# A Fourier-mixing and gated-MLP kernel on one core: moments in 32-byte pieces, merged down stores, and sums moved to the first stage

## The chip, the core and the metric

The kernel runs on one core of one Trainium2 chip. A core has a matrix engine (TensorE, PE in the profile, with its weight loads listed as PEld), a vector engine (VectorE, DVE), a scalar engine (ScalarE, ACT), a general engine (GpSimd, POOL) and a sync engine (SyncE, SP). SP and POOL issue nearly all transfers between the chip's memory and the core's buffers; the transfers themselves run on 16 DMA engines. The metric is device time in microseconds (us) of one execution; the median of three runs before the change is 836.01 us (834.29 to 838.94).

## The reference

With x of 2048 rows and 512 columns, in single precision:

```
xn = (x - mean(x)) / sqrt(var(x) + 1e-5)           # over the 512 columns
a, b = xn @ dft_hid_re.T, xn @ dft_hid_im.T        # 512 x 512 matrices
s  = dft_seq_re @ a - dft_seq_im @ b               # 2048 x 2048 matrices
h  = sigmoid(xn @ w_gate) * (xn @ w_up)            # 512 x 1792 each
g  = silu(h @ w_down)                              # 1792 x 512
out = x + s * g
```

All matrices are inputs; nothing is taken to be a Fourier matrix by its values.

## The kernel before

**Arithmetic.** A single-precision product is made of three matmuls on a rounded high part and the rest: high by high, high by low, low by high (`mm3`, L66). ACT makes the high part by a copy to the rounded type (L118), DVE the low part by a subtraction (L123). On top of that each large product is done as a 2 x 2 block product in seven instead of eight multiplications; the sums of blocks which that needs are made on DVE (`combine`, L127). The seven products carry the numbers 1 to 7. Operand data lies in 54 buffers of 4 KB per partition, called pages. A page is given out again when its last reader is done, so a store that has not landed keeps its page.

**Stages.** The work is a list of units, 12 matmuls of 512 columns each, or 18 where a product of the down projection rides along. Two units before a unit runs, its operands are split; five units before, they are loaded. Helper work is hung on unit numbers: `sooner` ahead of the unit, `after` behind it, `amid` between. Each engine takes its instructions in the order so written, and so do the SP and POOL queues.

1. Sequence transform (units 0 to 111): four chunks of 512 output rows. Chunks 0 and 1 share their first two products, unit by unit, while x is loaded, its row moments are computed (`stats`, L156) and x is normalised in place (`normalise`, L173). `stats` runs two statistics instructions on DVE for a tile, then on POOL variance plus epsilon, the power -1/2, the negated mean and the bias. The `moments` go to memory for later use (`store_moments`, L178) in eight transfers of single floats. The results, 16 blocks, go to memory as `f_raw` (L273).
2. Gate and up, with down (98 units from number n = 112): 14 blocks, each a half of the 2048 rows by a 256-wide group of hidden columns. `x_norm` (L424) normalises the transposed x with moments that are read back and broadcast to all partitions (L433, 16 instructions of 1024 columns). The seven down products of a block ride on the units that follow, in the order 2, 1, 6, 7, 4, 5, 3, into two `pd` banks. After each, `gather` (L473) copies both banks to a page on ACT (L477) and POOL stores the page to `g_part` in memory, adding to what is there (L479, or L482 where it is the first). Products 2 and 1 go to the same `g_part`.
3. Hidden transform and output (28 units): it multiplies sums of `f_raw` blocks by sums of the hidden matrices, then scales by silu of `g_part` and adds to the output. The sums are made during stage 2 and go through memory: `f_sums` (L640) at units n+40, n+52, n+64 and n+76, `w_sums` (L660) at n+84. Each `f_sums` loads four blocks, makes four sums on DVE and stores four; `w_sums` likewise. Left-over down products ride along here too.

Of the kernel before, what the change touches and what calls it, by code (L numbers as in the profile page):

```python
# [8 lines left out]
F32 = mybir.dt.float32  # L9
F32R = mybir.dt.float32r  # L10
AF = mybir.ActivationFunctionType
ALU = mybir.AluOpType
# [20 lines left out]
def fnet_glu_kernel(ctx: ExitStack, tc: tile.TileContext, x, x_t, c_re, c_im, w_h, w_gu, w_down, out):  # L33
# [122 lines left out]
    def stats(j, pp):  # L156
        mv = stat.tile([P, 2, 2], F32, name="mv")
        rs = stat.tile([P, 2], F32, name="rs")
        each = [slice(0, 1), slice(1, 2)] if pp == j == 0 else [slice(0, 2)]
        for e in range(2):  # L160
            st = stat.tile([P, 6], F32, name="st")
            nc.vector.bn_stats(st, xs[j, pp][:, e, :])
            nc.vector.bn_aggr(mv[:, e, :], st)
        for at in each:
            scale = moments[:, 1, pp, at, j]
            nc.gpsimd.tensor_scalar(rs[:, at], mv[:, at, 1], EPS, None, op0=ALU.add)
            nc.gpsimd.tensor_tensor(scale, rs[:, at], mhalf[:, at], op=ALU.pow)
        mean, scale, bias = (moments[:, m, pp, :, j] for m in range(3))
        nc.gpsimd.tensor_scalar(mean, mv[:, :, 0], -1.0, None, op0=ALU.mult)
        nc.gpsimd.tensor_tensor(bias, mean, scale, op=ALU.mult)  # L170
        return mv

    def normalise(j, pp, es=(0, 1), d=None):  # L173
        for e in es:
            v = xs[j, pp][:, e, :] if d is None else a_block(d, j, pp)[:, e]
            nc.scalar.activation(v, v, AF.Identity, scale=moments[:, 1, pp, e, j : j + 1], bias=moments[:, 2, pp, e, j : j + 1])
# [48 lines left out]
    class Chunk:  # L225
# [29 lines left out]
        def run(self, k, pp):  # L255
            ch = CHAIN[k]
            if k in (1, 5) and pp == 0:
                self.chain(ch)
            wv, xv = aop[k, pp].get(), self.op[k, pp].get()
            order = [(d, e) for d in range(2) for e in range(2)]  # L260
            if (k, pp) == (1, 0) and self.t < 2:
                order.sort(key=lambda v: v[1])
            late = (self.t, k, pp) == (1, 1, 0)
            for lows in ((0, 1), (2,)) if late else ((0, 1, 2),):
                for d, e in order:
                    ws = [v[:, e, d * P : (d + 1) * P] for v in wv]
                    first, last = k in (1, 5) and pp == e == 0, pp == 3 and e == 1
                    mm3(self.ps[ch, d], ws, [v[:, e, :] for v in xv], first, last, k not in (1, 5), late, lows)
            if pp == 3:
                self.done(k)  # L270

# [43 lines left out]
    def begin_seq():  # L315
        tags = ("a", "b", "pd"), ("c", "pd", "a"), ("b", "pd", "a"), ("c", "a", "pd")
        chunks = [Chunk(t, dict(zip("abc", tags[t])), t in (1, 2)) for t in range(NT)]
        for i, k in enumerate((1, 2)):
            for pp in range(4):
                for c in chunks[:2]:  # L320
                    add(c.needs(k, pp), lambda c=c, k=k, pp=pp: c.run(k, pp))
                m = 8 * i + 2 * pp
                if m > 4:
                    sooner(m - 6, lambda i=i, pp=pp: fetch(i, pp))
                if m > 2:
                    sooner(m - 4, lambda i=i, pp=pp: stats(i, pp))
                    sooner(m - 2, units[m][0][1].get)
                    sooner(m - 2, lambda i=i, pp=pp: normalise(i, pp))
                if i:
                    after(m + 2, lambda pp=pp: store_moments(pp))  # L330
        for k in (1, 2):
            chunks[2].add_product(k)
        for pp in range(4):
            m = 9 + 2 * pp
            after(m, lambda pp=pp: a_sums(pp, (1,)))
            after(m + 1, lambda pp=pp: a_sums(pp, (3,)))
            after(m + 2, aop[5, pp].get)
            after(m + 3, lambda pp=pp: a_sums(pp, (2,)))
            after(m + 4, lambda pp=pp: a_sums(pp, (4,)))
        for c in chunks[:3]:  # L340
            for k in (5, 6, 7, 3, 4):
                c.add_product(k)
        for k in (1, 5, 6, 3, 7, 2, 4):
            chunks[3].add_product(k)
        return chunks

    def begin(chunks):
        for i, tag in enumerate(("gb", "ub", "pd", "pd")):
            idle = bank(tag)
            for _ in range((4, 4, 1, 1)[i]):  # L350
                nc.tensor.matmul(idle, ones[:, :P], ones, start=True, stop=True)
        c = chunks[0].op[1, 0]
        raw = c.loads[0]
        raw.at = page(raw.shape, F32)
        for e in range(2):
            fetch(0, 0, (e,))
            nc.sync.dma_start(raw.at[:, e, :], raw.src[:, e, :])
# [10 lines left out]
        first = a_block(0, 0, 0)  # L368

        def normed(e):  # L370
            scale = moments[:, 1, 0, e, 0:1]
# [52 lines left out]
    def x_norm(h, b, at):  # L424

        c = 2 * h + b
        both = Load(m_part[c].rearrange("m t -> (m t)").partition_broadcast(P).rearrange("p (m t) -> p m t", m=2), [2, SB])
        raw = [Load(x_t[c * 2 + j], [2, SB]) for j in range(2)]

        def step(j, m):  # L430
            v = xraw[h, j, b] = raw[j].load()
            by = both.load()[:, m, :].unsqueeze(1).to_broadcast([P, 2, SB])
            nc.vector.tensor_tensor(v, v, by, op=(ADD, ALU.mult)[m])  # L433
# [36 lines left out]

    begun = set()

    def gather(i, outs, sign=1):  # L473

        pg = page([2, SB], F32)
        for o, po in enumerate(outs):
            nc.scalar.activation(pg[:, o, :], po, AF.Copy, scale=float(sign))  # L477
        if i in begun:
            nc.gpsimd.dma_start(g_part[i], pg, accum_op=ADD)  # L479
        else:  # L480
            begun.add(i)
            nc.gpsimd.dma_start(g_part[i], pg)  # L482


    SEVEN = (2, 1, 6, 7, 4, 5, 3)
    waiting = []
# [29 lines left out]
    class Seven:  # L516
# [37 lines left out]
        def run(self, k):  # L554
            first = k in (2, 1, 5)
            if first:
                self.ps = [bank("pd") for _ in range(2)]
            hv, wv = self.h[k].get(), self.weights(k)
            for o, ps in enumerate(self.ps):
                mm3(ps, [t[:, o * P : (o + 1) * P] for t in wv], hv, first, True, go_on=not first)  # L560
            (b, i), sign = {
                2: ((0, 0), 1),
                1: ((0, 0), 1),
                6: ((1, 0), -1),
                7: ((1, 1), -1),
                4: ((0, 1), 1),
                5: ((1, 1), 1),
                3: ((1, 0), 1),
            }[k]
            gather(self.first + 2 * b + i, self.ps, sign)  # L570
# [66 lines left out]

    SLOT = (5, 7, 6, 4)

    def f_sums(pair, half, at):  # L640

        a0, b0 = (Load(f_raw[2 * pair][2 * (half ^ 1) + j], [2, SB]) for j in range(2))
        a1, b1 = (Load(f_raw[2 * pair + 1][2 * (half ^ 1) + j], [2, SB]) for j in range(2))
# [9 lines left out]
            nc.gpsimd.dma_start(f_sum[pair][half][i], combine(dst(), a.get(), b.get(), ADD))  # L653

        for i, v in zip((0, 0, 1, 3), (a0, a1, b1, b0)):
            sooner(at + i - 3, v.load)
        for i, v in enumerate(steps):
            after(at + i, lambda i=i, v=v: step(i, *v))
# [153 lines left out]
    with tc.manual_schedule():  # L812
# [96 lines left out]
```

## Time and profile before

| | before |
|---|---|
| median of the runs | 836.01 us |
| profiled execution | 830.84 us |
| its span, first to last instruction | 829.1 us |
| mean granted clock | 0.991 |
| PE busy | 799.4 us (96%) |
| DVE busy | 668.1 us (81%) |
| ACT busy | 523.6 us (63%) |
| POOL busy | 141.9 us (17%) |
| mean transfer rate | 220 GB/s |

The span begins with the first instruction and ends with the last; what lies outside it makes up the difference to the execution's time. Times in the views count from the start of the span. Busy shares are averages over stages with different limits, so the views by stretch of time tell more than the page's totals.

### The profile page before, as it was taken

The numbers are of one execution on the slowest core, as the hardware profiler recorded it, in microseconds if no ns is written. First come the engines' busy times: TensorE is split into PE (matmuls) and PEld (weight loads), VectorE is DVE, ScalarE is ACT, GpSimd is POOL, SyncE is SP. The second block draws the span as 40 slices with busy tenths as digits, with TensorE's granted clock in tenths as the row PEclk, the third lists the DMA queues.
The fourth block names the chain that finished last, engine by engine and source line by source line (L and its number), as shares of the span: only waits on it lengthen the run. The fifth ranks groups of instructions, "written<-read, shape, count | busy, mean of one in ns | idle before, by whom it ended". The sixth has DMA issues, their size and how long they took to land.

```text
span 829.1 us, 9918 instructions
## 1 busy us (share of the span) xinstructions
PE 799.4 (96%) x3466; PEld 651.0 (79%) x3466; DVE 668.1 (81%) x851; ACT 523.6 (63%) x802; POOL 141.9 (17%) x195
## 2 busy tenths in 40 slices
PE   7999899999999999999999999999999899999996
PEld 5778678888888888888888787888888687767775
DVE  5798799878698798889999777677669798875856
ACT  4774564534525456588788758667677677876461
POOL 3350001000000000012222131222313112211301
PEclk8999999999999999999999999999999999999998
DMA  9929428296485337069987997999998999999996
GB/s 341 383 68 192 109 101 308 74 310 223 153 310 198 101 127 223 32 186 220 200 157 127 245 210 230 218 263 269 249 301 213 286 279 251 313 265 309 292 341 109
DMA packets 52625, 182.07 MB, mean 220 GB/s; under 512 B 5984, under 2 KB 6240, under 8 KB 52576
## 3 DMA queue, kind: packets, MB, share of 16 engines
q0 software_dynamic: 22464, 77.62, 43.4%
q1 hardware_dynamic: 30032, 103.76, 35.5%
q8 instruction: 27, 0.44, 0.2%
q14 instruction: 22, 0.18, 0.1%
q10 hardware_dynamic: 80, 0.07, 0.0%
HBM read 106.95 MB, written 78.14 MB: 223 GB/s over the span
## 4 chain that ended last, share of the span: by engine, by line
PE 58%; DMA 24%; DVE 6%; issue 5%; POOL 3%; ACT 3%; SPq 0%; POOLq 0%; DVEq 0%; ACTq 0%
DMA g_part<-page 16%; PE pd L70 14%; PE ga L70 11%; PE ua L70 11%; PE uc L70 7%; PE gc L70 7%; PE gb L70 4%; PE ub L70 4%; DMA page<-in_c_im_dram 3%; DVE page L123 3%; DMA page<-g_part 2%; DMA out_dram<-page 2%; ACT page L118 2%; POOL g_part L479 1%; DVE page L127 1%
## 5 line engine op out<-in xcount | busy, mean ns | idle before, releaser
L123 DVE TENSOR_TENSOR page<-page 128x512 fp32r<-128x512 f32 (+1 forms) x384 | 349.8, 939 | 92.3 <-ACT page L118 85.9
L118 ACT ACTIVATE page<-page 128x512 fp32r<-128x512 f32 (+1 forms) x384 | 303.5, 831 | 146.3 <-DVE page L127 106.7
L70 PE MATMUL pd<-page 128*128 128x512 f32 (+1 forms) x984 | 241.2, 388 | 8.8 <-DVE page L123 4.5
L70 PEld LDWEIGHTS pd<-page 128*128 128x128 f32 x984 | 182.7, 188 | 50.8 <-DVE page L123 5.9
L127 DVE TENSOR_TENSOR page<-page 128x1024 f32<-128x1024 f32 (+2 forms) x252 | 204.8, 834 | 14.2 <-DMA g_part<-page 8.7
L70 PE MATMUL ga<-page 128*128 128x512 f32 x600 | 156.5, 395 | 9.1 <-ACT page L583 4.0
L70 PE MATMUL ua<-page 128*128 128x512 f32 x600 | 155.7, 395 | 0.0
L70 PEld LDWEIGHTS ga<-page 128*128 128x128 f32 x600 | 111.9, 189 | 37.8 <-ACT page L583 5.0
L477 ACT ACTIVATE page<-pd 128x512 f32<-128x512 f32 x196 | 112.3, 597 | 44.4 <-PE pd L70 30.9
L70 PEld LDWEIGHTS ua<-page 128*128 128x128 f32 x600 | 115.0, 192 | 24.3
L479 POOL DMA_DIRECT2D g_part<-page x90 | 79.8, 977 | 296.9 <-ACT page L477 124.0
L70 PE MATMUL gc<-page 128*128 128x512 f32 x384 | 98.2, 390 | 0.0
L70 PE MATMUL uc<-page 128*128 128x512 f32 x384 | 97.9, 389 | 0.0
L70 PEld LDWEIGHTS gc<-page 128*128 128x128 f32 x384 | 72.4, 189 | 15.2
L70 PEld LDWEIGHTS uc<-page 128*128 128x128 f32 x384 | 72.1, 188 | 15.0
L70 PE MATMUL gb<-page 128*128 128x512 f32 x252 | 65.7, 393 | 3.1 <-DVE page L123 2.9
L70 PE MATMUL ub<-page 128*128 128x512 f32 x252 | 64.0, 389 | 0.0
L70 PEld LDWEIGHTS gb<-page 128*128 128x128 f32 x252 | 46.7, 188 | 15.5 <-DVE page L123 5.0
L70 PEld LDWEIGHTS ub<-page 128*128 128x128 f32 x252 | 47.3, 188 | 9.9
L273 POOL DMA_DIRECT2D f_raw<-page x16 | 8.8, 551 | 256.4 <-DVE page L285 182.1
L601 DVE TENSOR_TENSOR page<-page 128x512 f32<-128x512 f32 x28 | 19.3, 690 | 8.7 <-ACT page L598 7.7
L598 ACT ACTIVATE page<-page 128x512 f32<-128x512 f32 x28 | 17.6, 629 | 7.9 <-DVE page L593 7.8
(86 smaller groups left out, 319.7 us busy)
## 6 DMA issues: line engine op xcount, KB each, us to landing
g_part<-page POOLq DMA_DIRECT2D x98, 512.0 KB, 8.1
page<-in_c_re_dram SPq DMA_DIRECT2D x47, 512.0 KB, 5.5
page<-in_c_im_dram SPq DMA_DIRECT2D x32, 512.0 KB, 7.1
page<-f_raw SPq DMA_DIRECT2D x28, 512.0 KB, 9.2
page<-in_w_gu_dram SPq DMA_DIRECT2D x22, 512.0 KB, 7.1
f_raw<-page POOLq DMA_DIRECT2D x16, 512.0 KB, 6.1
f_sum<-page POOLq DMA_DIRECT2D x16, 512.0 KB, 8.2
page<-f_sum SPq DMA_DIRECT2D x16, 512.0 KB, 14.4
```

What stands on the lines that cost most here:

```text
L70: nc.tensor.matmul(ps, ws[w], ms[m], start=first and i == 0, stop=last and i == 2, skip_group_check=go_on)
L118: nc.scalar.activation(self.parts[0], self.raw, AF.Copy)
L123: nc.vector.tensor_tensor(lo, self.raw, hi.bitcast(F32), op=SUB)
L127: (engine or nc.vector).tensor_tensor(dst, a, b, op=op)
L273: nc.gpsimd.dma_start(f_raw[self.t][block], v)
L477: nc.scalar.activation(pg[:, o, :], po, AF.Copy, scale=float(sign))
L479: nc.gpsimd.dma_start(g_part[i], pg, accum_op=ADD)
L598: nc.scalar.activation(s[k][:, 0, :], ps["g" + tag] if tag else s[k][:, 0, :], AF.Sigmoid)
L601: nc.vector.tensor_mul(s[k][:, 0, :], s[k][:, 0, :], ps["u" + tag] if tag else s[k][:, 1, :])
```

## The change

1. `moments` has its axes swapped, so that the mean and the scale of one tile lie next to each other; one transfer per tile stores both in pieces of 32 bytes. `x_norm` reads them back in that order: its broadcast operand is now read with a step of 32 bytes instead of one element after the other.
2. In `stats`, variance plus epsilon (except for the first tile) and the negated mean are made on DVE. In the stage's second half the fetch and the statistics are hung one unit sooner.
3. At the start, both halves of the first x tile are issued ahead of the first transform block, and the second x tile ahead of the two blocks that follow. The second tile is normalised first in the half that product 1 needs; the other halves follow behind units 4 and 5. Two idle matmuls are added to the warm-up.
4. In the units of products 1 and 2 of chunks 0 and 1 (all but one), the eight matmuls that need one of the low parts come first and the four that need the other come behind them; for chunk 1 the low part of x goes first.
5. The down product 2 is copied to a page by ACT as before, product 1 is added to that page by DVE (two instructions on 512 columns), and the page is stored once.
6. `f_sums` of the first pair moves to units n-46 and n-35, in the first stage, one step every two units; that of the second pair to n+54 and n+66; `w_sums` to n+46.

```diff
-    moments = const.tile([P, 3, 4, 2, 2], F32, name="moments")
-    m_part = [dram.tile([2, SB], F32, name=f"m_part{i}") for i in range(NT)]
+    moments = const.tile([P, 4, 3, 2, 2], F32, name="moments")
+    m_part = [dram.tile([P, 2, 4], F32, name=f"m_part{i}") for i in range(NT)]
...
+        mean, scale, bias = (moments[:, pp, m, :, j] for m in range(3))
...
-        for at in each:
-            scale = moments[:, 1, pp, at, j]
-            nc.gpsimd.tensor_scalar(rs[:, at], mv[:, at, 1], EPS, None, op0=ALU.add)
-            nc.gpsimd.tensor_tensor(scale, rs[:, at], mhalf[:, at], op=ALU.pow)
-        mean, scale, bias = (moments[:, m, pp, :, j] for m in range(3))
-        nc.gpsimd.tensor_scalar(mean, mv[:, :, 0], -1.0, None, op0=ALU.mult)
+        if pp or j:
+            nc.vector.tensor_scalar(rs, mv[:, :, 1], EPS, None, op0=ALU.add)
+            nc.gpsimd.tensor_tensor(scale, rs, mhalf, op=ALU.pow)
+        nc.vector.tensor_scalar(mean, mv[:, :, 0], -1.0, None, op0=ALU.mult)
...
     def store_moments(b):
-        for m in range(2):
-            nc.gpsimd.dma_start(m_part[b][m].rearrange("(o p) -> p o", p=P), moments[:, m, b].rearrange("p e j -> p (e j)"))
+        nc.gpsimd.dma_start(m_part[b], moments[:, b, 0:2].rearrange("p m e j -> p m (e j)"))
...
-            late = (self.t, k, pp) == (1, 1, 0)
-            for lows in ((0, 1), (2,)) if late else ((0, 1, 2),):
+            split_up = self.t < 2 and k in (1, 2) and (self.t, k, pp) != (0, 1, 0)
+            for lows in ((0, 1), (2,)) if split_up else ((0, 1, 2),):
...
-                    sooner(m - 6, lambda i=i, pp=pp: fetch(i, pp))
+                    sooner(m - (6, 7)[i], lambda i=i, pp=pp: fetch(i, pp))
...
-                    sooner(m - 4, lambda i=i, pp=pp: stats(i, pp))
+                    sooner(m - (4, 5)[i], lambda i=i, pp=pp: stats(i, pp))
...
-            for _ in range((4, 4, 1, 1)[i]):
+            for _ in range((4, 4, 2, 2)[i]):
...
         for e in range(2):
             fetch(0, 0, (e,))
+        for e in range(2):
             nc.sync.dma_start(raw.at[:, e, :], raw.src[:, e, :])
-        units[1][0][1].load()
         fetch(0, 1)
-        units[2][0][1].load()
+        for n in (1, 2):
+            units[n][0][1].load()
...
-        normalise(0, 1)
+        normalise(0, 1, d=0)
         aop[1, 1].get()
-        for e in range(2):
-            after(3, lambda e=e: normalise(0, 0, (e,), 1))
+        for pp in range(2):
+            after(4 + pp, lambda pp=pp: normalise(0, pp, d=1))
...
-            by = both.load()[:, m, :].unsqueeze(1).to_broadcast([P, 2, SB])
-            nc.vector.tensor_tensor(v, v, by, op=(ADD, ALU.mult)[m])
+            to = v.rearrange("k i (o p) -> k i o p", o=4)
+            by = both.load()[:, :, m, :].rearrange("k p o -> k o p").unsqueeze(1).to_broadcast([P, 2, 4, P])
+            nc.vector.tensor_tensor(to, to, by, op=(ADD, ALU.mult)[m])
...
+            if k == 2:
+                self.part = page([2, SB], F32)
+                for o, ps in enumerate(self.ps):
+                    nc.scalar.activation(self.part[:, o, :], ps, AF.Copy)
+                return
+            if k == 1:
+                for o, ps in enumerate(self.ps):
+                    nc.vector.tensor_add(self.part[:, o, :], self.part[:, o, :], ps)
+                return keep(self.first, self.part)
...
-        for p in range(2):
-            for half in range(2):
-                f_sums(p, half, n + 40 + 12 * (2 * p + half))
-        w_sums(n + 84)
+        f_sums(0, 0, n - 46, 2)
+        f_sums(0, 1, n - 35, 2)
+        f_sums(1, 0, n + 54, 1)
+        f_sums(1, 1, n + 66, 1)
+        w_sums(n + 46)
```

Here `keep` is the store half of the old `gather`: POOL's transfer to `g_part`, adding where the block is not the first.

More of the change, by code (lines that the diff above doesn't have):

```diff
@@ L158, in stats @@
         rs = stat.tile([P, 2], F32, name="rs")
-        each = [slice(0, 1), slice(1, 2)] if pp == j == 0 else [slice(0, 2)]
+        mean, scale, bias = (moments[:, pp, m, :, j] for m in range(3))
         for e in range(2):
@@ L163, in stats, with normalise @@
             nc.vector.bn_aggr(mv[:, e, :], st)
-        for at in each:
-            scale = moments[:, 1, pp, at, j]
-            nc.gpsimd.tensor_scalar(rs[:, at], mv[:, at, 1], EPS, None, op0=ALU.add)
-            nc.gpsimd.tensor_tensor(scale, rs[:, at], mhalf[:, at], op=ALU.pow)
-        mean, scale, bias = (moments[:, m, pp, :, j] for m in range(3))
-        nc.gpsimd.tensor_scalar(mean, mv[:, :, 0], -1.0, None, op0=ALU.mult)
+            if pp == j == 0:
+                nc.gpsimd.tensor_scalar(rs[:, e : e + 1], mv[:, e, 1:2], EPS, None, op0=ALU.add)
+                nc.gpsimd.tensor_tensor(scale[:, e : e + 1], rs[:, e : e + 1], mhalf[:, e : e + 1], op=ALU.pow)
+        if pp or j:
+            nc.vector.tensor_scalar(rs, mv[:, :, 1], EPS, None, op0=ALU.add)
+            nc.gpsimd.tensor_tensor(scale, rs, mhalf, op=ALU.pow)
+        nc.vector.tensor_scalar(mean, mv[:, :, 0], -1.0, None, op0=ALU.mult)
         nc.gpsimd.tensor_tensor(bias, mean, scale, op=ALU.mult)
         return mv
-    def normalise(j, pp, es=(0, 1), d=None):
-        for e in es:
+    def normalise(j, pp, d=None):
+        for e in range(2):
             v = xs[j, pp][:, e, :] if d is None else a_block(d, j, pp)[:, e]
-            nc.scalar.activation(v, v, AF.Identity, scale=moments[:, 1, pp, e, j : j + 1], bias=moments[:, 2, pp, e, j : j + 1])
+            nc.scalar.activation(v, v, AF.Identity, scale=moments[:, pp, 1, e, j : j + 1], bias=moments[:, pp, 2, e, j : j + 1])
     def store_moments(b):
-        for m in range(2):
-            nc.gpsimd.dma_start(m_part[b][m].rearrange("(o p) -> p o", p=P), moments[:, m, b].rearrange("p e j -> p (e j)"))
+        nc.gpsimd.dma_start(m_part[b], moments[:, b, 0:2].rearrange("p m e j -> p m (e j)"))
     def a_block(d, j, pp):
@@ L267, in run @@
                     first, last = k in (1, 5) and pp == e == 0, pp == 3 and e == 1
-                    mm3(self.ps[ch, d], ws, [v[:, e, :] for v in xv], first, last, k not in (1, 5), late, lows)
+                    mm3(self.ps[ch, d], ws, [v[:, e, :] for v in xv], first, last, k not in (1, 5), self.t == 1, lows)
             if pp == 3:
@@ L356, in begin @@
             fetch(0, 0, (e,))
+        for e in range(2):
             nc.sync.dma_start(raw.at[:, e, :], raw.src[:, e, :])
-        units[1][0][1].load()
         fetch(0, 1)
-        units[2][0][1].load()
+        for n in (1, 2):
+            units[n][0][1].load()
         fetch(0, 2)
@@ L370, in normed @@
         def normed(e):
-            scale = moments[:, 1, 0, e, 0:1]
+            scale = moments[:, 0, 1, e, 0:1]
             nc.vector.tensor_scalar(first[:, e], first[:, e], mv[:, e, 0:1], scale, op0=SUB, op1=ALU.mult)
@@ L426, in x_norm @@
         c = 2 * h + b
-        both = Load(m_part[c].rearrange("m t -> (m t)").partition_broadcast(P).rearrange("p (m t) -> p m t", m=2), [2, SB])
+        both = Load(m_part[c].rearrange("p m o -> (p m o)").partition_broadcast(P).rearrange("k (p m o) -> k p m o", m=2, o=4), [P, 2, 4])
         raw = [Load(x_t[c * 2 + j], [2, SB]) for j in range(2)]
@@ L471, in fnet_glu_kernel, with keep @@
     begun = set()
[L473 to L477, printed above, removed]
+    def keep(i, pg):
         if i in begun:
@@ L482, in gather @@
             nc.gpsimd.dma_start(g_part[i], pg)
+    def gather(i, outs, sign=1):
+        pg = page([2, SB], F32)
+        for o, po in enumerate(outs):
+            nc.scalar.activation(pg[:, o, :], po, AF.Copy, scale=float(sign))
+        keep(i, pg)
     SEVEN = (2, 1, 6, 7, 4, 5, 3)
@@ L560, in run @@
                 mm3(ps, [t[:, o * P : (o + 1) * P] for t in wv], hv, first, True, go_on=not first)
+            if k == 2:
[7 more added lines that the diff above has]
+                return keep(self.first, self.part)
             (b, i), sign = {
-                2: ((0, 0), 1),
-                1: ((0, 0), 1),
                 6: ((1, 0), -1),
@@ L638, in fnet_glu_kernel, with f_sums @@
     SLOT = (5, 7, 6, 4)
-    def f_sums(pair, half, at):
+    def f_sums(pair, half, at, gap=1):
         a0, b0 = (Load(f_raw[2 * pair][2 * (half ^ 1) + j], [2, SB]) for j in range(2))
@@ L655, in f_sums @@
         for i, v in zip((0, 0, 1, 3), (a0, a1, b1, b0)):
-            sooner(at + i - 3, v.load)
+            sooner(at + gap * i - 3, v.load)
         for i, v in enumerate(steps):
-            after(at + i, lambda i=i, v=v: step(i, *v))
+            after(at + gap * i, lambda i=i, v=v: step(i, *v))
     def w_sums(at):
```

## The prediction

> **What bounds the kernel now.** I read the page's totals first, then the busy time by stretch, then PE's order of time, the chain and the waits.
>
> ```profile
> span 829.1 us, 9918 instructions
> PE 799.4 (96%) x3466; PEld 651.0 (79%) x3466; DVE 668.1 (81%) x851; ACT 523.6 (63%) x802; POOL 141.9 (17%) x195
> ```
>
> ```profile
> core 0: us, PE busy (x) PEld busy (x) DVE busy (x) ACT busy (x) POOL busy (x), PEclk, DMA share, GB/s
> 0.00:50.00 50.00, 42.93 (x156) 31.90 (x156) 34.05 (x59) 31.28 (x43) 20.04 (x38) 0.93 0.82 315
> 50.00:92.00 42.00, 39.22 (x170) 31.51 (x170) 33.32 (x40) 23.25 (x31) 8.51 (x13) 1.00 0.76 139
> 92.00:336.00 244.00, 244.00 (x1076) 201.14 (x1075) 213.77 (x208) 121.04 (x145) 12.12 (x20) 1.00 0.54 186
> 336.00:464.00 128.00, 128.00 (x566) 106.02 (x565) 118.93 (x179) 104.08 (x180) 22.09 (x28) 1.00 0.74 156
> 464.00:640.00 176.00, 174.71 (x769) 143.86 (x769) 128.27 (x191) 124.63 (x223) 43.09 (x57) 1.00 0.96 248
> 640.00:700.00 60.00, 55.57 (x236) 44.91 (x235) 48.69 (x73) 41.51 (x75) 13.71 (x18) 0.97 0.98 271
> 700.00:780.00 80.00, 75.10 (x320) 59.16 (x319) 61.20 (x76) 60.51 (x92) 17.15 (x19) 1.00 1.05 296
> 780.00:829.00 49.00, 39.90 (x184) 32.47 (x182) 29.84 (x34) 17.28 (x20) 5.21 (x5) 0.95 0.89 235
> ```
>
> PE is the bound, and what a change can win is what each stretch loses against back-to-back matmuls. In the undisturbed stretch, 92 to 336, 1076 matmuls take 244.0 us, 0.2267 us each. By that price the first 50 us hold 146 matmuls of work (10 of the 156 are warm-up) = 33.1 us and lose 16.9; 50 to 92 loses 42 - 170 x 0.2267 = 3.5; 92 to 464 loses nothing; 464 to 640 loses 1.7; 640 to 700 loses 6.5; 700 to 780 loses 7.5. The last stretch loses some 10 us (24 of its 184 matmuls are half as wide), mostly the tail behind the last matmul.
>
> ```profile
> 7.69 1.25 PE L70 MATMUL ga<-page 128*128 128x512 f32 x3 [2.12 <-ACT page L375]
> 16.91 2.10 PE L70 MATMUL ga<-page 128*128 128x512 f32 x6 [1.83 <-ACT page L118]
> 91.57 5.53 PE L70 MATMUL pd<-page 128*128 128x512 f32 x23 [2.78 <-DVE page L123]
> 655.48 1.85 PE L70 MATMUL ga<-page 128*128 128x512 f32 x6 [3.65 <-ACT page L583]
> ```
>
> Of the 16.9 us, 7.7 lie ahead of the first matmul; the stall at 16.9 (1.8 us) is followed by slow matmuls (granted clock 0.93 in the stretch). The chain tells what stands behind the stalls:
>
> ```profile
> 9.61 0.62 DVE st L162
> 10.25 0.18 DVE mv L163
> ...
> 11.32 1.13 POOL rs L166
> 12.53 1.54 POOL moments L167
> 14.13 0.24 POOL moments L169
> 14.44 0.20 POOL moments L170
> 15.39 0.81 ACT page L176
> 25.67 1.08 ACT page L176 x2
> ...
> 63.38 25.75 DMA page<-in_c_im_dram
> 640.86 17.61 DMA g_part<-page
> ```
>
> ```profile
> g_part<-page POOLq DMA_DIRECT2D x98, 512.0 KB, 8.1
> page<-in_c_im_dram SPq DMA_DIRECT2D x32, 512.0 KB, 7.1
> m_part<-moments POOLq DMA_DIRECT2D x8, 2.0 KB, 15.5
> ```
>
> So the stall at 16.9 is statistics, four small POOL operations and a normalisation in a row. The stall at 91 is one ordinary 512 KB load that took 25.75 us, while eight stores of 2 KB, issued just before, took 15.5 us each at the median. The late stalls are stores to `g_part`:
>
> ```profile
> POOL g_part L479 <- DMA g_part<-page: 51.5, 5, 16.2
> ACT page L118 <- DMA g_part<-page: 21.1, 14, 4.5
> ```
>
> POOL stands five times, 51.5 us in all, until an earlier `g_part` store has landed, since adding to the same block must wait; its other stores queue behind it, their pages stay taken, and ACT waits for pages 14 times.
>
> **The change, part by part.**
>
> *Start.* On the chain of the second tile the first POOL operation (1.13 us) and the third (0.24) become DVE operations near the statistics' aggregation in size (0.18), one beside the power: 1.2 us less. Normalising one half only takes two 256-column operations (1.08 us together, from 25.67) instead of two of 0.81: 0.5 less. x arrives a little sooner, as the two x halves are no longer interleaved with the block, and the block's first half one place later; I take 0.5 us on the first matmul. The 512 KB block of unit 1 goes behind the second x tile, another 512 KB, some 1.6 us at the 315 GB/s of this stretch; PE is still at unit 0, which hides it; uncovered it costs those 1.6. The split matmul order costs no instruction and gives each late low part eight matmuls (1.8 us) more. Without the stall the slow matmuls behind it (about 2 us) go too. Sum: 0.5 + 1.7 + 2 = 4.2, and 1.8 more from the same shortening and the earlier statistics at the later tiles: 6.0 of the 9.2 lost behind the first matmul. Bounds: 2 (if transfers set the pace; their share is 0.82) and 9. POOL loses some 15 operations; DVE gains 15 of about 0.2 us, 3 us of the 50 - 34 it has free; nothing on POOL's queue waits longer.
>
> *Moments in memory.* Eight transfers of 512 pieces become four of 128. At an eighth of the pieces the crowd around 63 to 89 should be gone; if the time goes by bytes, nothing is won. Bounds 0 and 3.5; I take 3.0, since no row but these 2 KB stores explains 25.75 us for a load whose kind takes 7.1 at the median. POOL issues four fewer, ahead of the two `f_raw` stores. If the load at 91 is ready, the next late thing is unknown; the stretch behind it has no loss.
>
> *Reading the moments back* (L433, DVE) now steps 32 bytes. No row shows such a read; the nearest is the same operation unstepped:
>
> ```profile
> L433 DVE TENSOR_TENSOR page<-page 128x1024 f32<-128x1024 f32 x16 | 19.5, 1219 | 0.0
> L593 DVE TENSOR_TENSOR page<-page,gc 128x512 f32<-128x512 f32 x28 | 19.1, 681 | 2.0 <-ACT page L583 1.8
> ```
>
> I take 1.22 us, no change, and carry twice that in the rivals. The Trainium skill speaks against the change here: "SBUF — State Buffer", section "Door 1: The DMA port swizzle", says that SBUF lines have 16 bytes and that each access which crosses to a new line pays a penalty. By that rule every element of this operand pays; no run here shows it so far.
>
> *One store for products 2 and 1.* ACT loses 28 copies (L477), DVE gains 28 additions out of PSUM like L593, 0.68 us each: 19 us over 14 blocks. Where does DVE have room? From 336 to 464 it is busy 118.93 of 128 and gains four blocks x 2 x 0.68 = 5.4: 97%. Product 6 may not overwrite the banks until the addition is done. At its worst place of these four:
>
> ```profile
> 440.26 1.52 PE L70 MATMUL pd<-page 128*128 128x512 f32 x6
> 443.19 1.29 DVE L127 TENSOR_TENSOR page<-page 128x512 f32<-128x512 f32 x2
> 444.34 1.52 PE L70 MATMUL pd<-page 128*128 128x512 f32 x6
> ```
>
> Product 1 ends at 441.6, DVE comes to the addition's place at 443.2, would end at 444.5, and product 6 starts at 444.34: a wait of some 0.2 us. Elsewhere there is over 1 us to spare. With DVE's backlog I take a loss of 1 us, bounds 0 and 5.4 (nothing absorbed). POOL and the DMA engines lose 14 stores, and the pair that had to follow one another on one block 4.1 us apart (18 x 0.2267) with a landing of 8.1 is gone.
>
> ```profile
> q0 software_dynamic: 7632, 27.79, 72.0%
> q1 hardware_dynamic: 4319, 15.73, 24.1%
> ...
> g_part<-page POOLq DMA_DIRECT2D x43, 512.0 KB, 8.3
> page<-f_raw SPq DMA_DIRECT2D x14, 512.0 KB, 7.7
> f_sum<-page POOLq DMA_DIRECT2D x14, 512.0 KB, 8.2
> ```
>
> *Sums moved.* This is the queue view of 464 to 640. 72% of 176 us for 57 stores is 2.2 us of all engines for one; 24.1% over 30 loads (15.73 MB at 512 KB) is 1.4. The first pair's sums (8 loads, 8 stores, 29 us of transfers) leave for units 66 to 83, where the share was 0.54; with 8 additions of 1.22 on DVE, which had 30 of 244 us free there: cost nothing, and up to 1.5 if they bunch with the normalisation at units 76 to 83. `w_sums` (14 us) comes 38 units earlier, from 640 to 700 into 464 to 640, which also sheds six merged stores (13). So 464 to 640 goes from 169 us of transfers to about 145, 640 to 700 from 59 to about 38 (w_sums, two late `f_sum` stores, two merged). The loads and stores of the moved sums pass the chunk's own on SP and POOL; their sources, stored at unit 63 or before, are read at 63 and 74.
>
> With transfers down from 96-98% to 82 and 63%, the 1.7 us (I take 1.4) and the 6.5 us (6.0) should go. From 700 to 780 the share is 1.05 and the stage's own loads stay; what it sheds is backlog, two merged stores and POOL's waits: 3.0 of 7.5, bounds 0 and 6. Late sum 10.4, bounds 3 and 13.
>
> *Sum.* 6.0 + 3.0 - 1.0 + 10.4 = 18.4 us. The profiled execution, 830.84 (span 829.1 and 1.7 around it), becomes 812.4. It ran 5.2 us under the median of the runs, 836.01; against that median the time is 817.6.
>
> **Rivals.**
>
> - *Stepped reads hold up DVE.* If L433 doubles, 8 such operations fall into 336 to 464: 9.8 us more on a DVE with 9.1 - 5.4 = 3.7 to spare, so PE waits about 6, and up to 2 more near unit 80. Time 817.6 + 8 = 825.6. Against it only that nothing in the rows shows a step to cost. It is the mechanism that the Trainium skill's rule on lines would give.
> - *The late stage stays bound by transfers*: what is moved comes back as other backlog, and 10.4 us are not won: 828.0. For it speaks the 1.05 of 700 to 780; against it that the merged stores and the pair's wait vanish rather than move.
> - *The addition of product 1 becomes the wait* (the slower side). PE waits in each of 14 blocks from the point where DVE starts the addition over 4.08 - 1.36 - 1.28 = 1.4 us after the product ends; 3.6 us late costs 2.2 x 14 = 30: 847.6. It takes over 1.6 us a block, a start over 3 us late, to make the kernel slower by 0.5%. The rows show 1.6 us late at the worst place, so the chance is small.
> - *The 4-byte pieces are not the cause* of the load at 63: 3.0 less is won, 820.6; this lies inside the forecast's range.
>
> **How the numbers follow.** Forecast 0.62 (with the last rival), stepped reads 0.16, transfer-bound late stage 0.11, the addition 0.11. 0.5% (4.2 us: below 831.8 or above 840.2) is about what a measurement of this kernel can tell from no change. Forecast is all faster; of the second case 0.13 are faster, of the third 0.07, the rest same; the fourth is slower: faster 0.82, same 0.07, slower 0.11. The forecast's own range is 810 (start 9, late 13, DVE 0) to 824; to hold 8 in 10 it takes in the second and most of the third rival: 809 to 833.
>
> **What would show it.** Right: the first 50 us with over 165 matmuls; no PE gap near 90, and `m_part` stores landing in a few us; no POOL wait of 10 us or more on a `g_part` store before 700; 640 to 700 with about 262 matmuls in 60 us; L433 still 1.22 us. Wrong: L433 near 2.4 and PE waiting on DVE around 400 to 464; matmuls on `pd` waiting for the new addition in every block; new PE gaps near 200 to 260, where the first pair's sums now lie; or the same gaps from 690 to 780 with the transfer share still at 1.

## The result

| | before | after |
|---|---|---|
| median of the runs | 835.15 us (4 runs, 834.21 to 838.94) | 810.25 us (4 runs, 809.88 to 810.86) |
| profiled execution | 830.84 us | 810.13 us |
| its span | 829.1 us | 808.3 us |

The ratio is 0.9694, with a 95% interval of 0.9662 to 0.9726: 3.1% faster. It lies within the range given (809 to 833), 1.3 us above its lower end, and 7.4 us under the predicted 817.6.

The busy time of the changed kernel by the same stretches of time (columns as before: PE, PEld, DVE, ACT, POOL with their instruction counts, granted clock, share of the DMA engines, rate):

```profile
core 0: us, PE busy (x) PEld busy (x) DVE busy (x) ACT busy (x) POOL busy (x), PEclk, DMA share, GB/s
0.00:50.00 50.00, 44.46 (x184) 35.11 (x184) 41.75 (x82) 37.92 (x53) 17.86 (x26) 1.00 0.86 328
50.00:92.00 42.00, 42.00 (x187) 34.79 (x186) 38.81 (x43) 24.20 (x32) 2.69 (x5) 1.00 0.44 149
92.00:336.00 244.00, 241.71 (x1065) 199.34 (x1064) 224.03 (x215) 119.35 (x143) 16.42 (x28) 1.00 0.61 218
336.00:464.00 128.00, 124.20 (x541) 100.63 (x540) 125.74 (x178) 93.50 (x164) 19.53 (x24) 1.00 0.67 140
464.00:640.00 176.00, 175.11 (x771) 144.41 (x771) 134.66 (x203) 121.44 (x214) 36.49 (x48) 1.00 0.90 227
640.00:700.00 60.00, 60.00 (x266) 49.69 (x266) 52.16 (x83) 46.40 (x80) 10.39 (x12) 1.00 0.89 210
700.00:780.00 80.00, 80.00 (x355) 66.21 (x354) 61.85 (x74) 58.47 (x83) 15.26 (x16) 1.00 1.04 291
780.00:829.00 49.00, 22.47 (x111) 18.89 (x109) 20.50 (x25) 9.34 (x10) 3.60 (x3) 0.96 0.42 104
```

At 0.2267 us a matmul the losses are as follows (12 warm-up matmuls taken off the first stretch; the last stretch runs from 780 to the end of the span and holds 24 matmuls of half width in both kernels; a matmul that lies across a boundary counts on both sides, so a loss is good to some 0.3 us):

| stretch | lost before | lost after | gained | forecast |
|---|---|---|---|---|
| 0 to 50 | 16.9 | 11.0 | 5.9 | 6.0 |
| 50 to 92 | 3.5 | 0 | 3.5 | 3.0 |
| 92 to 464 | 0 | 7.9 | -7.9 | -1.0 |
| 464 to 640 | 1.7 | 1.2 | 0.5 | 1.4 |
| 640 to 700 | 6.5 | 0 | 6.5 | 6.0 |
| 700 to 780 | 7.5 | 0 | 7.5 | 3.0 |
| 780 to the end | 10.1 | 5.9 | 4.2 | 0 |
| sum | 46.2 | 26.0 | 20.2 | 18.4 |

The spans differ by 20.8. So the sum came out nearly as forecast, but by larger terms of both signs, which is luck. The new loss begins at the read-back of the moments; the group, the first new gap in PE's order of time, and the stores of the moments and of `g_part`, all of the changed kernel:

```profile
L435 DVE TENSOR_TENSOR page<-page 128x1024 f32<-128x1024 f32 x16 | 34.2, 2138 | 0.0
```

```profile
236.68 1.43 PE L70 MATMUL gb<-page 128*128 128x512 f32 x5 [2.01 <-DVE page L123]
```

```profile
m_part<-moments POOLq DMA_DIRECT2D x4, 4.0 KB, 4.8
```

```profile
POOL g_part L477 <- DMA g_part<-page: 8.0, 1, 8.0
```

L435 is L433 of before: 2.14 us instead of 1.22. The stores of the moments land in 4.8 us instead of 15.5, and POOL waits once, 8.0 us, for a `g_part` store, where it waited five times, 51.5 us in all.

### The profile page after: what moved, and what is told of

Same layout as the page of the kernel before. It is cut to its first block, busy times and chain, and to the rows that moved or that the text cites. A ratio compares the mean times of both kernels' runs of the same rounds, so it can differ in the third digit from the quotient of the medians.

```text
span 808.3 us, 9885 instructions
## 1 busy us (share of the span) xinstructions
PE 789.9 (98%) x3468; PEld 649.1 (80%) x3468; DVE 699.5 (87%) x894; ACT 510.6 (63%) x776; POOL 122.2 (15%) x162
## 4 chain that ended last, share of the span: by engine, by line
PE 59%; issue 27%; DMA 6%; DVE 4%; POOL 3%; ACT 1%; SPq 0%; POOLq 0%; DVEq 0%; ACTq 0%
PE pd L70 18%; PE ga L70 11%; PE ua L70 11%; PE uc L70 6%; PE gc L70 6%; DMA g_part<-page 4%; PE ub L70 4%; PE gb L70 4%; POOL g_part L477 2%; DVE page L127 1%; DVE page L123 1%; DMA f_raw<-page 1%; DMA page<-in_c_re_dram 1%; DVE st L162 0%; POOL f_raw L273 0%
## 5 line engine op out<-in xcount | busy, mean ns | idle before, releaser
L70 PE MATMUL ga<-page 128*128 128x512 f32 x600 | 154.2, 391 | 6.9 <-ACT page L118 2.9
L70 PE MATMUL ua<-page 128*128 128x512 f32 x600 | 153.0, 389 | 0.0
L70 PEld LDWEIGHTS ua<-page 128*128 128x128 f32 x600 | 112.6, 188 | 23.5
L477 POOL DMA_DIRECT2D g_part<-page x76 | 66.4, 874 | 281.1 <-ACT page L486 160.7
L486 ACT ACTIVATE page<-pd 128x512 f32<-128x512 f32 x140 | 81.4, 599 | 23.4 <-PE pd L70 16.1
L435 DVE TENSOR_TENSOR page<-page 128x1024 f32<-128x1024 f32 x16 | 34.2, 2138 | 0.0
```

Source lines behind the costliest of these rows:

```text
L70: nc.tensor.matmul(ps, ws[w], ms[m], start=first and i == 0, stop=last and i == 2, skip_group_check=go_on)
L435: nc.vector.tensor_tensor(to, to, by, op=(ADD, ALU.mult)[m])
```

## The experiments

Each edit is against the changed kernel, unless it says against the kernel before. Kernels are compared by their own medians, since the median of the kernel before, which ratios divide by, moved from 832.1 to 835.2 us between the sets of runs. The changed kernel was timed in the first set alone, so a difference of under some 3 us from a kernel of another set is not settled by the medians; there the stretches of the profiles decide.

**Part 1 undone** (single floats, read back without a step).

```diff
-        nc.gpsimd.dma_start(m_part[b], moments[:, b, 0:2].rearrange("p m e j -> p m (e j)"))
+        for m in range(2):
+            nc.gpsimd.dma_start(m_part[b][m].rearrange("(o p) -> p o", p=P), moments[:, m, b].rearrange("p e j -> p (e j)"))
...
-            by = both.load()[:, :, m, :].rearrange("k p o -> k o p").unsqueeze(1).to_broadcast([P, 2, 4, P])
+            by = both.load()[:, m, :].unsqueeze(1).to_broadcast([P, 2, SB])
```

> The changed kernel with part 1 alone undone: moments stored as single floats in eight transfers and read back one element after the other. If the 32-byte step is what made L435 2.14 us, the read-back is 1.22 us again and the stalls of the changed kernel between 92 and 464 us (8.8 us of PE time in the windows) shrink to 2 us or less. If DVE's additions for product 1 and the first pair's sums cause them, at least 5 us of them stay. If the single floats caused the slow load, a PE gap of some 2 to 3 us near 85 us comes back; if that gap was a matter of the start's timing, it does not. By my theory the two nearly cancel: 810.3 - 7 + 3 = 806 us; by the rival on the additions 812 us.

Measured: 803.59 us (801.97 to 806.98), under the changed kernel by 6.7. The read-back's group, the chain, PE's order of time, the stores of the moments, and busy time by stretch:

```profile
L435 DVE TENSOR_TENSOR page<-page 128x1024 f32<-128x1024 f32 x16 | 19.5, 1219 | 0.0
```

```profile
53.17 26.43 DMA page<-in_c_im_dram
```

```profile
82.04 9.78 PE L70 MATMUL pd<-page 128*128 128x512 f32 x35 [2.92 <-DVE page L123]
```

```profile
m_part<-moments POOLq DMA_DIRECT2D x8, 2.0 KB, 18.0
```

```profile
92.00:336.00 244.00, 243.00 (x1073) 200.95 (x1072) 218.99 (x216) 120.58 (x145) 16.42 (x28) 1.00 0.60 218
336.00:464.00 128.00, 127.51 (x563) 105.26 (x562) 123.21 (x183) 98.50 (x171) 19.53 (x24) 1.00 0.67 146
```

Both halves of the expectation came; the time is 2.4 us under the 806 expected. Without the step the loss from 92 to 464 is 1.1 us instead of 7.9. With single floats one 512 KB load takes 26.43 us again and PE stands 2.92 us, at another time and behind another start than in the kernel before; in this execution, the slowest of the four, 50 to 92 loses 4.6 us. So part 1 wins the gap and loses more than that in DVE time.

**The step itself.** The four tiles' moments in pieces of 32, 16, 8 and 4 bytes:

```diff
-    m_part = [dram.tile([P, 2, 4], F32, name=f"m_part{i}") for i in range(NT)]
+    PIECE = (8, 4, 2, 1)
+    m_part = [dram.tile([8 // PIECE[i], P, PIECE[i]], F32, name=f"m_part{i}") for i in range(NT)]
```

> The changed kernel with the four tiles' moments stored in pieces of 32, 16, 8 and 4 bytes, so that DVE reads them back with a step of 32, 16, 8 and 4 bytes (the 8-byte one as two operations of half the size, whose unstepped time is 0.68 us each). If lines of 16 bytes decide, 32 and 16 bytes take 2.14 us and 8 and 4 bytes 1.22 us (0.68 a half). If any step costs, 8 bytes is slower than 0.68 a half as well; if the price grows with the step, 16 bytes lies between 1.22 and 2.14.

The groups of DVE, in the order 32, 16, 8 and 4 bytes (one run, 803.48 us):

```profile
L439 DVE TENSOR_TENSOR page<-page 128x1024 f32<-128x1024 f32 x4 | 8.5, 2134 | 0.0
L442 DVE TENSOR_TENSOR page<-page 128x1024 f32<-128x1024 f32 x4 | 8.0, 1998 | 0.0
L446 DVE TENSOR_TENSOR page<-page 128x512 f32<-128x512 f32 x8 | 5.2, 685 | 0.0
L449 DVE TENSOR_TENSOR page<-page 128x1024 f32<-128x1024 f32 x4 | 4.9, 1217 | 0.0
```

A step of 8 bytes costs nothing (685 ns, beside 681 to 690 of unstepped operations of that size); 16 bytes cost 64% and 32 bytes 75%, so most of the price comes at once and a little grows with the step. In a step of 8 bytes two elements share a line of 16 bytes, in one of 16 each has its own. The rule of the Trainium skill that was weighed in the prediction ("SBUF — State Buffer", section "Door 1: The DMA port swizzle") says that at least two hits a line are needed for the full rate, and the runs agree with that. The same note of the Trainium skill goes on to call a stride of up to 4 single-precision elements free; the step of 16 bytes, 4 such elements, costs 64% here, and the measurement decides.

**Part 5 undone** (products 2 and 1 stored separately).

```diff
-            if k == 2:
-                self.part = page([2, SB], F32)
...
-                return keep(self.first, self.part)
             (b, i), sign = {
+                2: ((0, 0), 1),
+                1: ((0, 0), 1),
```

> The changed kernel with part 5 alone undone: products 2 and 1 copied by ACT and stored separately. If the wait of the second store on the first was what cost the late stage, POOL waits of 8 us or more on g_part stores return and 464 to the end loses 6 us or more again, while DVE is 19 us less busy and 336 to 464 loses 2 us instead of 3.8: about 815 us. If the earlier sums alone freed the late stage, the late stage still loses under 2 us and the time falls to about 808 us.

Measured: 822.03 us (817.14 to 828.18), slower than the changed kernel by 11.8 and 7 us slower than expected. POOL's waits and three stretches:

```profile
POOL g_part L477 <- DMA g_part<-page: 71.3, 7, 15.0
```

```profile
92.00:464.00 372.00, 368.53 (x1620) 303.45 (x1619) 347.60 (x386) 217.85 (x318) 40.02 (x57) 1.00 0.65 200
464.00:740.00 276.00, 269.76 (x1177) 221.47 (x1177) 202.38 (x300) 204.85 (x357) 59.70 (x75) 0.99 0.94 233
740.00:780.00 40.00, 35.98 (x155) 28.54 (x154) 27.15 (x28) 21.96 (x29) 9.99 (x10) 1.00 1.04 298
```

From 464 to 780 it loses 9.2 + 4.9 = 14.1 us, although the sums lie at their new units. The earlier sums alone do not free the late stage.

**Part 5 alone**, on the kernel before, by the lines that the diff of part 5 adds.

> The kernel before with part 5 alone: product 1 added by DVE to product 2's page, one store for both. If the merge is the whole late gain, 464 to the tail loses under 4 us instead of 19, nothing else moves, and 336 to 464 loses at most 1 us: about 16 us faster than the kernel before, ratio 0.981. If the late gain needs the earlier sums or the earlier start as well, at least 8 of the 19 us stay lost: ratio 0.990 or more.

Measured: 810.62 us (809.39 to 811.85), ratio 0.9727 (0.9696 to 0.9758): nearly as good as the whole change (0.9694), whose other parts are absent. By stretch:

```profile
92.00:464.00 372.00, 371.51 (x1636) 306.41 (x1635) 336.01 (x393) 219.70 (x315) 31.08 (x44) 1.00 0.57 168
464.00:740.00 276.00, 274.92 (x1208) 226.15 (x1208) 227.60 (x335) 197.91 (x344) 58.91 (x78) 1.00 0.98 261
740.00:780.00 40.00, 40.00 (x178) 33.12 (x177) 28.95 (x31) 25.57 (x33) 7.43 (x7) 1.00 1.07 294
```

464 to 780 loses 2.1 us (276 - 1208 x 0.2267, and nothing after 740), with the DMA engines at 0.98 and 1.07, as busy as ever. The 28 additions cost 1.1 us from 92 to 464 while the read-back is unstepped. It won 22 us against the expected 16.

**The wait or the number of stores?** On the kernel before, product 1 adds to a block of its own:

```diff
-            gather(self.first + 2 * b + i, self.ps, sign)
+            gather(2 * NT + self.first // 4 if k == 1 else self.first + 2 * b + i, self.ps, sign)
```

> The kernel before with product 1 added to a block of memory of its own (one for each quarter of the rows) and not to product 2's; the final g then lacks product 1's share, all else is computed. The number of stores and of adding stores, ACT's copies and DVE's work stay as before; only the wait of product 1's store for product 2's is gone. If that wait is the cause of the late loss, POOL's waits on g_part stores fall from 51 to under 15 us and 464 to the tail loses under 6 us instead of 19: ratio 0.984 or less. If the number of transfers is the cause, the late loss stays above 13 us: ratio 0.993 or more.

Measured: 819.99 us (816.74 to 821.29), ratio 0.9839 (0.9805 to 0.9872). Two of the 98 stores no longer add, since each new block begins with one. Waits and stretches of it, then the same stretches of the kernel before:

```profile
ACT page L118 <- DMA page<-w_part: 6.6, 2, 3.9
ACT page L118 <- DMA page<-in_w_h_dram: 6.3, 1, 6.3
POOL g_part L479 <- DMA g_part<-page: 12.9, 2, 9.6
```

```profile
464.00:740.00 276.00, 275.68 (x1214) 227.33 (x1214) 215.59 (x314) 212.20 (x366) 67.50 (x88) 1.00 1.02 271
740.00:780.00 40.00, 34.77 (x141) 26.68 (x140) 25.78 (x27) 18.08 (x22) 6.57 (x6) 0.96 1.06 304
```

```profile
464.00:740.00 276.00, 267.01 (x1158) 217.44 (x1158) 210.51 (x310) 198.56 (x349) 63.07 (x83) 0.99 0.98 261
740.00:780.00 40.00, 38.36 (x165) 30.49 (x165) 27.63 (x29) 28.10 (x39) 10.87 (x12) 1.00 1.05 287
```

The ratio and POOL's waits are those of the first expectation; the late loss lies between the two. With the wait gone and all 98 stores kept, 464 to 740 loses 0.8 us where the kernel before loses 13.5 by the same count (1158 matmuls in 276 us). But 740 to 780 now loses 8.0 (2.6 before), where ACT waits for loads of the hidden matrices and of their sums. So the wait is the cause up to 740, and taking it out alone is worth 12.7 us of the merge's 22. That the rest comes from the transfers, which the merge thins as well, is likely but not shown: no run thins the stores and keeps the wait.

**Part 6 undone** (sums at their old units).

> The changed kernel with part 6 alone undone: f_sums and w_sums at their old units. If transfers moved out of 464 to 700 were the late gain, 464 to 780 loses 6 us or more again, and the stall near 237 us (2.2 us) goes: about 814 us. If merging the stores was enough, the late stage stays within 2 us of loss and the time falls by the 2.2 us of the stall near 237 to about 808 us.

Measured: 806.47 us (806.30 to 807.70), under the changed kernel by 3.8. The stretches of the moved sums:

```profile
92.00:336.00 244.00, 244.00 (x1076) 201.57 (x1076) 217.60 (x211) 119.56 (x145) 12.17 (x20) 1.00 0.52 183
464.00:640.00 176.00, 175.74 (x776) 145.15 (x775) 138.63 (x207) 117.94 (x209) 38.92 (x53) 1.00 0.95 242
640.00:700.00 60.00, 59.61 (x262) 48.72 (x261) 57.95 (x90) 47.58 (x85) 12.82 (x17) 1.00 1.04 290
700.00:780.00 80.00, 80.00 (x355) 66.20 (x354) 60.14 (x68) 58.68 (x82) 14.20 (x15) 1.00 1.05 305
```

The stall near 237 is gone, and the late stage loses 0.6 us at a DMA share of 1.04 to 1.05. Once the stores are merged, moving the sums wins 0.6 us after 640 and loses 2.5 in the first stage. From 464 to 640 the changed kernel loses 1.1 more (1.2 against 0.1), but of five other profiled kernels with the moved sums and the merge four lose at most 0.3 there. The stall near 237 needs the stepped read-back too: with part 1 undone and the sums moved it is 1.00 us instead of 2.01. About a microsecond of the 3.8 lies in the start, which differs by that much from execution to execution (0 to 50 loses 9.9 us here and 9.9 to 11.0 in the kernels with the whole new start, the changed kernel's profiled execution at the upper end). By the ratios, 0.9697 and 0.9694, the two kernels are the same; the stretches say that moving the sums does not pay.

**Parts 2, 3 and 4 undone.**

> The changed kernel with parts 2, 3 and 4 undone: statistics on POOL, old order of the first loads, two warm-up matmuls fewer, old matmul order. Everything else as changed. By my account these parts were worth 6.0 us of the first 50 us (15.0 lost by 60 us before, 8.5 after); so about 816 us, with the stall near 16 us and the slow matmuls behind it back, and no gap near 88 us. If the pieces of 32 bytes helped the start too, it is less than 6.0 slower.

Measured: 816.15 us (815.15 to 816.91), 5.9 over the changed kernel, against 6.0 worked out. The old stall is back, with slow matmuls behind it, and no gap near 88:

```profile
17.41 2.10 PE L70 MATMUL ga<-page 128*128 128x512 f32 x6 [1.83 <-ACT page L118]
```

**Of the start, the two operations alone and the warm-up alone.**

> The changed kernel with variance plus epsilon and the negated mean on POOL again for all tiles; the orders of loads, units and matmuls and the warm-up stay changed. If the two small POOL operations were 1.2 us of the second tile's chain, the matmul that starts at 14.8 us starts 1.2 us later, and the third tile's at 22.0 us some 2 us later; if the load order and the half normalisation did it all, both starts stay within 0.5 us.

> The changed kernel with ten warm-up matmuls instead of twelve. If the two extra ones keep PE at full clock through the wait for the first tile, the first unit's matmuls are 0.43 us each again and the first 20 us lose about 1.7 us more than the changed kernel's 6.8. If the shorter wait for the first tile does that alone, the loss stays within 0.6 us of it.

PE's order of time of the changed kernel, then with the statistics' two small operations on POOL again, then without the extra warm-up matmuls:

```profile
6.83 1.26 PE L70 MATMUL ga<-page 128*128 128x512 f32 x3 [1.05 <-ACT page L376]
...
14.84 1.19 PE L70 MATMUL ga<-page 128*128 128x512 f32 x4 [1.52 <-ACT page L118]
...
21.98 1.20 PE L70 MATMUL ga<-page 128*128 128x512 f32 x4 [1.41 <-ACT page L118]
```

```profile
15.43 1.20 PE L70 MATMUL ga<-page 128*128 128x512 f32 x4 [2.48 <-ACT page L118]
23.39 1.58 PE L70 MATMUL ga<-page 128*128 128x512 f32 x4 [2.22 <-ACT page L118]
```

```profile
6.45 1.26 PE L70 MATMUL ga<-page 128*128 128x512 f32 x3 [0.38 <-ACT page L376]
14.58 1.20 PE L70 MATMUL ga<-page 128*128 128x512 f32 x4 [1.38 <-ACT page L118]
```

With the operations on POOL the second tile's matmul comes 0.6 us later than in the changed kernel's execution (1.2 expected) and the third's 1.4 (2 expected); the single time is 813.0 us. But that execution is the latest one: in seven others with the same start (one of them without the extra warm-up) the two matmuls begin at 13.56 to 14.58 and at 20.70 to 21.73 us, and against those the delay is 0.9 to 1.9 and 1.7 to 2.7. On the chain itself, from the end of the second tile's statistics to its normalisation, the two executions take 3.5 and 2.6 us. So single executions do not settle the expected 1.2. Without the extra warm-up nothing is later (809.1 us): the wait for the first tile is short enough without it. The slow matmuls of before, 0.43 us each, followed a wait of 2.1 us.

**Both losses taken out, two ways.** The sums at their old units, and either ACT puts the moments in order once after they are read back, or they are stored in pieces of 8 bytes:

```diff
+        def turn():
+            flat = page([2, SB], F32)
+            for m in range(2):
+                nc.scalar.activation(flat[:, m, :].rearrange("k (o p) -> k o p", o=4), both.load()[:, :, m, :].rearrange("k p o -> k o p"), AF.Copy)
+            return flat
```

> The changed kernel with f_sums and w_sums at their old units, and with the moments put in order once by ACT after they are read back (two copies of 512 columns for each of the four tiles), so that DVE reads its operand one element after the other again; the 32-byte pieces stay. If the 32-byte step and the moved sums are the two losses of the change, L-form of the read-back is 1.22 us, 92 to 464 loses under 1 us, there is no gap near 88 us, and the time is 806.5 - 5.5 = 801 us. If the stalls of 336 to 464 come from DVE's additions instead, it stays at 806 us.

Measured: 803.47 us (802.54 to 804.24), ratio 0.9646 (0.9619 to 0.9672); the read-back takes 1.22 us again. From 92 to 464 it loses 2.0 us (556 matmuls from 336 to 464), not the under 1 expected, all from 336 to 464, and the time is 2.5 us over the 801 expected.

> The changed kernel with the moments stored in pieces of 8 bytes (256 a tile) and read back in two operations of half the size with a step of 8 bytes, and with f_sums and w_sums at their old units. If steps up to 8 bytes are free, as e8 says, 92 to 336 loses nothing, 336 to 464 about 0.7 us (against 2.2 with ACT's copies), there is no gap near 88 us as 256 pieces are a half of before's, and the time is 1 to 2 us under that of the version with ACT's copies: about 802 us. If 256 pieces a store are already too many, a gap of 1 us or more near 85 us comes back and it is no faster.

Measured: 802.60 us (801.30 to 804.05), ratio 0.9617 (0.9589 to 0.9646) to the kernel before. The stores of the moments and two stretches:

```profile
m_part<-moments POOLq DMA_DIRECT2D x4, 4.0 KB, 10.7
```

```profile
50.00:92.00 42.00, 42.00 (x187) 34.79 (x186) 38.75 (x43) 25.06 (x33) 3.15 (x5) 1.00 0.49 148
336.00:464.00 128.00, 127.28 (x561) 104.86 (x560) 122.45 (x190) 97.66 (x170) 20.10 (x25) 1.00 0.73 161
```

256 pieces a tile land in 10.7 us and hold up no load that PE waits for. This version is 7.65 us under the changed kernel; that it also beats the version with ACT's copies is within the spread of the two.

## Why the prediction was right, and where it was not

- *The start, 6.0 us*: right in size (5.9 by the stretches, 5.9 by undoing parts 2 to 4), though the start varies by a microsecond from execution to execution, so the agreement to a tenth is luck. Inside it, the two operations moved from POOL were weighed at 1.2 us on the second tile's chain; undoing them moved its matmul by 0.6 to 1.9, depending on the execution compared with. The two warm-up matmuls, which the sum gave no price, had none.
- *The moments' store, 3.0 us*: right in cause, and in size for the profiled execution. With single floats the slowest 512 KB load of this kind between 50 and 95 us took 22.1 to 26.4 us in four profiled kernels, whatever the start; with pieces of 32 bytes at most 8.4, of 8 bytes 11.6. The gap is gone with the larger pieces. With single floats it is there in three of the four (2.78 us before, 2.92 with part 1 undone, 1.88 with part 5 alone) and missing in the fourth (product 1 to a block of its own), where the slowest load took 22.1 us and came in time. So the 3.0 us are not won in every execution.
- *The read-back at 1.22 us, no change*: wrong. This is the step that failed. The first rival held: 2.14 us. It was taken at twice 1.22 and priced at 8 us of stalls; the stretch from 92 to 464 loses 7.9, and 1.1 without the step. It came about as that rival said, on a DVE that is busy 125.74 of 128 us from 336 to 464.
- *The additions of product 1, 1 us*: right where the read-back is unstepped (1.1 us with part 5 alone). Together with the step they cost more: from 336 to 464 the changed kernel loses 5.4 us, with the step but no additions about 2 us (4.7 from 92 to 464, of which 2.6 lie before 336), with the additions but no step 0.4. The rival's price of 6 us there counted both.
- *The sums moved, at no cost*: wrong by 2 to 3 us. The bunching with the read-back near unit 80, which was named with up to 1.5 us, came as a stall of 2.01 us at unit 82 (1.00 where the read-back is unstepped), and the relief that this part was to bring was not needed.
- *The late stage, 10.4 us*: right that it would be won, undersized, and in good part for another reason than the sum gave. The wait of product 1's store for product 2's was named, and it was the main cause. But 7.4 of the 10.4 us were to come from a transfer share that falls to 82% from 464 to 640 and to 63% from 640 to 700. It fell to 0.90 and 0.89 only, 7.0 us were won all the same, and with part 5 alone 464 to 740 loses just 2.1 us at a share of 0.98. The stretch from 700 to 780 was held back to 3.0 of 7.5 because its transfer share was 1.05; the share is still 1.04 and the stretch loses nothing. So a full set of DMA engines is no loss by itself; up to 740 the loss was in the POOL queue and the pages that stood behind one wait. The second rival, that the late stage stays bound by transfers, is refuted for the changed kernel; with the wait gone and all 98 stores kept, a part of it holds, as 740 to 780 then loses 8.0 us. The tail's 4.2 us were not forecast at all; they too belong to the merge, since from 780 to the end part 5 alone loses 5.8 us and the kernel with the wait taken out 6.3, against 10.1 before.
- *From the profiled execution to the median*: I carried over the 5.2 us by which the median stood above the profile. The changed kernel's median is 0.1 above its profile. The kernels with the pair's wait spread over some 10 us (828.25 to 836.57 in one set of runs of the kernel before, 817.14 to 828.18 without the merge), those without it over 1 to 5, though most of these in fewer runs (4 to 6, against 7 to 13). Of the 7.4 us of error 5.1 are this, and 2.3 (20.7 against 18.4 us between the profiled executions) the terms above.

The parts do not add up: part 5 alone is worth 22 us on the kernel before, and undoing it in the changed kernel costs 11.8. About 2 us of the difference come from its additions: they cost 3.2 us from 92 to 464 where the stepped read-back has filled DVE (7.9 against 4.7 lost), and 1.1 in the kernel before. The moved sums may help a kernel that still has the wait, but no run adds part 6 alone to the kernel before, so the rest stays open.

## What to carry to other kernels

Before stores to one place in memory are issued back to back with an addition in memory, add the values on the chip: here that alone was worth 22 us, more than all other parts together, and 12.7 of them came from the wait of the second store on the first in an in-order queue. When a layout is changed to make a transfer's pieces larger, look at the step with which compute engines read it afterwards, and choose the smallest piece that frees the transfer: 8 bytes did here, where half the operand was read in 0.685 us, as without a step. A share of 1.0 on the DMA engines says that they are busy, not that anybody waits for them; ask the waits.

## What the runs showed of the hardware that was not expected

- DVE's reading price jumps between a step of 8 bytes (0.685 us for 512 columns, as without a step) and one of 16 (2.00 us for 1024, against 1.22), and grows little after that (2.13 at 32 bytes).
- Stores of 2 KB in 512 single floats land in 14 to 18 us and an ordinary 512 KB load beside them takes 22 to 26 us, against at most 8.4 beside pieces of 32 bytes; 4 KB in 256 pieces of 8 bytes land in 10.7, in 128 pieces of 32 bytes in 4.8.
- PE runs without a gap from 640 to 780 us while the DMA engines are at a share of 0.89 to 1.04.
